# Window attention with a feed-forward layer on one core: six token tiles through DRAM instead of four, and a new table of the slices that carry scores, weight sums and saves

## The chip, the cores and the metric

One Trainium2 core does all of the work; the other cores of the chip stand idle. The time is the device time of one execution in microseconds. Three runs of the kernel before gave 850.49, 3289.97 and 848.82 us, and the median, 850.49 us, is its time. The program is written out in full for each engine: TensorE (PE) multiplies, VectorE (DVE), ScalarE (ACT) and GpSimd (POOL) work on tiles, and SyncE (SP) issues all DMAs. Each engine takes its instructions in the order in which the program names them, so an instruction that waits holds up all that stand behind it on its engine.

## The reference

Eight heads attend inside a window, four of them plain and four with dilation 4; a feed-forward layer with a leaky rectifier of its own slope for each hidden unit follows.

```python
B, H, S, D = 8, 8, 576, 64          # q, k, v are (8, 8, 576, 64)
scores = q @ k.T / sqrt(D)          # per batch and head
plain:   0 <= row - col < 32                                  (heads 0..3)
dilated: 0 <= row - col < 128 and (row - col) % 4 == 0         (heads 4..7)
attn = softmax(where(mask, scores, -1e9)) @ v
x = attn as (4608 tokens, 512)
h = x @ w_in                        # 512 -> 2048
g = max(h, 0) + alpha * min(h, 0)
out = g @ w_out                     # 2048 -> 512
```

## The kernel before, in words

The 4608 tokens form nine tiles of 512. Every fp32 operand of a big product is split into a high and a low part, and three passes (high by high, high by low, low by high) make one product.

**Two stages of the feed-forward layer.** Tiles 0 to 2 are done in 48 *slices*: slice n takes one tile and one block of 128 hidden units. In slice n TensorE does the input product of slice n+1 (line 488, `h`, 12 matmuls) and the output product of slice n-1 (line 536, `y`, 12 matmuls). Between them ScalarE and VectorE turn `h` into `m` (lines 496 and 501, or 508 and 509 on VectorE alone), then into its high part `g` (ACT, line 514) and its low part (DVE, line 519). Tiles 3 to 8 follow in a *paired stage*, which makes seven products out of eight (lines 729 and 1030) and needs sums of weight blocks for that. These sums are made during the slices: `combine` (line 586 and 589, POOL) for the input weights with its high part by ACT (line 594) and its low part by DVE (line 599), `others` (lines 616, 619, POOL; 624, ACT; 629, DVE) for the output weights. They are stored in DRAM, as are the plain weights (`save`, lines 568 to 572, four DMAs in each of 16 slices from `SCRATCH` on), and come back through a ring.

**The attention.** A *pair* is one batch element with two heads of one of four columns; there are 32. Pairs 8 to 23 are spread over the slices by the table `turns_at`: a pair's scores (PE line 266, 72 matmuls) are made in one slice, its values (PE line 361, 76 matmuls) in the slice of the next entry. Between the two stand the masks and maxima (DVE 318, 321), nine exponentials (ACT 331), the divisions (DVE 338, 339, 340) and the transpose into `pt` (DVE 346), which `values` waits for. The divisions stand in the slice after the scores. Where two entries are neighbours, all of that has one slice; else it has two. The result of `values` is copied to the token tiles, by ACT at lines 415 (between the fifth and the sixth exponential of the pair scored in that slice) and 422, for tiles 0 to 2 also by DVE (420).

**Where the tokens go.** For a tile in `KEPT` the copy goes to a small tile `kept_..` with the tag "m" (the five buffers of this tag also hold the `m` tiles, and the four output tiles `ob_..` of a token tile that is done), is stored to DRAM (line 225) and loaded again when its turn comes. Other tiles stay in SBUF (`raw_xA`, `raw_xB`). In the last slices `late_ops` prepare tiles 3 and 4 for the paired stage (`token_parts`: ACT 711, DVE 708 and 714).

**DMA.** SP issues every DMA in program order. The weights of the slices up to 21 are loaded by `load_weight` (line 435, tiles `ws`) in slices up to 18 and converted by ACT (457, 458, 473) and DVE (465, 467, 476). In slice 32 the output of token tile 0 is finished: four `ob` tiles are loaded with the first part (line 534), added to (DVE 544) and stored (line 549).

Of the kernel before, what the change touches and what calls it, by code (L numbers as in the profile page):

```python
# [8 lines left out]
F32 = mybir.dt.float32  # L9
# [8 lines left out]
P = 128  # L18
# [12 lines left out]
NTILE = NT // TT  # L31
NC = DM // P
NF = DFF // P
NSTD = 3
# [4 lines left out]
NRING = 10  # L39
HALF = 8  # L40
CUT = 6
KEPT = tuple(range(NSTD + 2, NTILE))
CHAINS = ((0, 5), (5, 5), (10, 4), (14, 4))


# [21 lines left out]
def tile_window_attention_prelu_ffn(  # L67
# [15 lines left out]
    const = ctx.enter_context(tc.tile_pool(name="const", bufs=1))  # L83
# [437 lines left out]
    def ffn_y(t, f):  # L521
        first = (t, f) in ((0, 0), (0, CUT), (1, 0), (2, HALF))
        if first:
            ys[t] = [bank("y", [P, TT], f"y_{t}_{f}_{c}") for c in range(NC)]
        g = gs.pop((t, f))
        cut, rest = (t, f) == (0, CUT - 1), t == 0 and f == NF - 1
        last = cut or (t, f) in ((0, NF - 1), (1, NF - 1), (2, HALF - 1))
        if last:
            o = [
                att.tile([P, TT], F32, tag=("k", "q", "v", "pt")[c], name=f"ob_{t}_{f}_{c}") if cut else  # L530
                ffp.tile([P, TT], F32, tag="m", name=f"ob_{t}_{f}_{c}", bufs=5) for c in range(NC)]
        for c in range(NC):
            if rest:
                nc.sync.dma_start(out=o[c], in_=part[c])
            for n, (a, e) in enumerate(PASSES):
                nc.tensor.matmul(  # L536
                    ys[t][c], lhsT=weight(1, a, f)[:, c * P:(c + 1) * P], rhs=g[:, e, :],
                    start=(first and n == 0), stop=(last and n == 2),
                )

        def end():
            for c in range(NC):
                if rest:
                    nc.vector.tensor_tensor(out=o[c], in0=ys[t][c], in1=o[c], op=ALU.add)
                elif c % 2:
                    nc.vector.tensor_copy(out=o[c], in_=ys[t][c])
                else:
                    nc.scalar.copy(out=o[c], in_=ys[t][c])
                nc.sync.dma_start(
                    out=part[c] if cut else outT[c * P:(c + 1) * P, t * TT:(t + 1) * TT], in_=o[c])  # L550

        if last:
            ended.append(end)
# [51 lines left out]

    wc = {}

    def others(i):

        if not ysums:  # L610
            ysums.append(const.tile([P, 2, 4, 2 * P], F32, tag="xA0", name="ysums"))
        t = ysums[0][:, len(ysums) % 2]
        ysums.append(t)
        for j in range(2):
            hi, lo = (weight(1, a, 2 * i + j).bitcast(F32) for a in range(2))
            nc.gpsimd.tensor_tensor(
                out=t[:, 2 * j:2 * j + 2].rearrange("p q n -> p (q n)"), in0=hi, in1=lo, op=ALU.add)
        for out, x, y, op in ((3, 1, 3, ALU.add), (1, 0, 1, ALU.subtract), (0, 3, 0, ALU.subtract), (2, 2, 0, ALU.subtract)):
            nc.gpsimd.tensor_tensor(out=t[:, out], in0=t[:, x], in1=t[:, y], op=op)
        sums_of[i] = t  # L620
# [13 lines left out]
                nc.sync.dma_start(  # L634
                    out=wY[i, q, :, :, a], in_=(t if a else t.bitcast(F32))[:, q].rearrange("p (c n) -> p c n", c=2))

    ysums = []
    sums_of = {}

    PRODUCTS = (1, 7, 6, 2, 5, 3, 4)  # L640
# [447 lines left out]

    def reload(t, c):
        tag = RAWTAGS[t]  # L1090
        if c == 0:
            cells.pop(tag, None)
            split.pop(tag, None)
        nc.sync.dma_start(out=half(t, c), in_=kept[t][c])
# [65 lines left out]
    def plan_parts():  # L1160
        zeroth, first, second = token_parts(NSTD)
        late_ops[NS - 9] = zeroth[:2]
        late_ops[NS - 5] = zeroth[2:] + first
        late_ops[NS - 3], late_ops[NS - 2], late_ops[NS - 1] = second[:5], second[5:8], second[8:]
# [3 lines left out]
    slices += [(2, f) for f in range(HALF, NF)] + [(2, f) for f in range(HALF)]  # L1168
    NS = len(slices)
    SECOND = CUT + NF  # L1170
    SCRATCH = CUT + NF - 2
    pairs = [Pair(b, c) for b in range(B) for c in range(NC)]


# [159 lines left out]
            ffn_y(*slices[n - 1])  # L1334

    score_at, value_at = {}, {}
    turns_at = (20, 22, 23, 24, 26, 27, 29, 30, 32, 33, 35, 36, 38, 40, 42, 44, 46)
    for p, (n, m) in enumerate(zip(turns_at, turns_at[1:]), 2 * NC):
        score_at[n] = pairs[p]
        value_at[m] = pairs[p]  # L1340
    divide_at = {n + 1: u for n, u in score_at.items()}

    split_at, combine_at = {}, {}
    for k, n in enumerate((21, 23, 25, 31, 33, 35, 37, 39)):
        combine_at[n] = (k + NFP // 2) % NFP
        split_at[n + 2] = combine_at[n]

    other_at, cast_at = {}, {}
    for k, n in zip((4, 5, 0, 1, 2, 3), range(32, 44, 2)):
        other_at[n] = cast_at[n + 2] = k  # L1350
    put = defaultdict(list)

    for n in range(CUT, NS):
# [69 lines left out]
        if n in cast_at:  # L1423
            others_low(cast_at[n])
            put[n + 1].append(lambda i=cast_at[n]: others_store(i))
        if n == HALF + 3:
            pairs[2 * NC].load_qk()
            pairs[2 * NC].load_v()
        for op in put.pop(n, ()):
# [3 lines left out]
        if n in combine_at:  # L1433
            combine(combine_at[n], "xB1" if n < 2 * NF - 1 else "xA1")
        if n in other_at:
            others(other_at[n])
        if n == NS - 9:
            plan_parts()
        if n == NS - 3:
            nc.sync.dma_start(out=mask_sb, in_=masks[:, NMASK:2 * NMASK])  # L1440
        for op in late_ops.pop(n, ()):
            op()
        if n >= NS - NRING + 2:
            feed()

    ffn_y(*slices[-1])
    ended.pop()()
    feed()
# [70 lines left out]
```

## Time and profile before

| what | us |
|---|---|
| runs | 850.49, 3289.97, 848.82 |
| median | 850.49 |
| the profiled execution | 849.21 |
| its span, first to last instruction | 846.7 |
| TensorE busy in the span | 823.8 (97%) |
| VectorE busy | 651.2 (77%) |
| ScalarE busy | 466.2 (55%) |
| GpSimd busy | 89.9 (11%), all but 0.2 of it from 163 us on to 363 us |

The slices 20 to 47 lie between about 163 and 363 us of the span, the paired stage behind them. A table by stretches of the span shows for each stretch how long each engine was busy; what TensorE is short of the stretch's length is time that it waited. A timeline row gives the start, the length, the engine, the line, the operation with the tile it writes and those it reads, and, in square brackets, how long the engine had been idle before it and what released it.

### The profile page before, as it was taken

The numbers are of one execution on the slowest core, as the hardware profiler recorded it, in microseconds if no ns is written. First come the engines' busy times: TensorE is split into PE (matmuls) and PEld (weight loads), VectorE is DVE, ScalarE is ACT, GpSimd is POOL, SyncE is SP. The second block draws the span as 40 slices with busy tenths as digits, with TensorE's granted clock in tenths as the row PEclk, the third lists the DMA queues.
The fourth block names the chain that finished last, engine by engine and source line by source line (L and its number), as shares of the span: only waits on it lengthen the run. The fifth ranks groups of instructions, "written<-read, shape, count | busy, mean of one in ns | idle before, by whom it ended". The sixth has DMA issues, their size and how long they took to land.

```text
span 846.7 us, 20417 instructions
## 1 busy us (share of the span) xinstructions
PE 823.8 (97%) x8014; PEld 670.0 (79%) x8014; DVE 651.2 (77%) x1088; ACT 466.2 (55%) x1275; POOL 89.9 (11%) x88
## 2 busy tenths in 40 slices
PE   8899999999999999999999999999999999999997
PEld 5677888887878777787888788878887888888886
DVE  5987767668668887879966999897289988934983
ACT  7885766554545655657436752665176436624640
POOL 0000000205054896000000000000000000000000
PEclk9999999999999999999999999999999999999999
DMA  7853444179889988695898599866876886767664
GB/s 256 273 176 112 131 163 148 45 250 303 274 256 301 289 272 261 189 298 167 260 317 300 158 323 302 259 185 198 250 212 193 288 291 192 194 193 195 191 195 150
DMA packets 137918, 190.71 MB, mean 225 GB/s; under 512 B 11870, under 2 KB 78046, under 8 KB 137822
## 3 DMA queue, kind: packets, MB, share of 16 engines
q1 hardware_dynamic: 137822, 189.41, 71.7%
q8 instruction: 63, 1.03, 0.5%
q14 instruction: 33, 0.27, 0.1%
HBM read 143.23 MB, written 46.14 MB: 224 GB/s over the span
## 4 chain that ended last, share of the span: by engine, by line
PE 79%; DVE 12%; ACT 4%; issue 2%; DMA 2%; SPq 0%; ACTq 0%; DVEq 0%
PE h L488 15%; PE qA L1030 15%; PE y L536 13%; PE pA L729 11%; PE qC L1030 7%; PE pC L729 6%; PE qB L1030 4%; PE pB L729 3%; PE o L361 3%; PE s L266 2%; ACT pr L331 2%; DVE held L788 1%; DVE pr L340 1%; DVE gp L843 1%; DVE stage L781 1%
## 5 line engine op out<-in xcount | busy, mean ns | idle before, releaser
L488 PE MATMUL h<-x,w_dt.float32r 128*128 128x512 f32 x576 | 143.5, 398 | 4.1 <-issue 1.7
L536 PE MATMUL y<-g,w_dt.float32r 128*128 128x512 f32 x576 | 138.5, 389 | 0.0
L488 PEld LDWEIGHTS h<-x,w_dt.float32r 128*128 128x128 f32 x576 | 107.6, 190 | 28.5 <-issue 2.6
L536 PEld LDWEIGHTS y<-g,w_dt.float32r 128*128 128x128 f32 x576 | 108.0, 188 | 22.5
L331 ACT ACTIVATE pr<-pr,nm 128x64 f32<-128x64 f32 x216 | 72.5, 339 | 33.5 <-DVE nm L321 30.7
L774 ACT COPY stage<-pA 128x512 f32<-128x512 f32 x72 | 42.3, 587 | 47.6 <-PE pA L729 46.9
L729 PE MATMUL pA<-parts_w,ring_w 128*128 128x512 f32 x234 | 58.1, 391 | 0.2 <-ACT stage L774 0.2
L838 ACT CAST gp<-held 128x512 fp32r<-128x512 f32 x60 | 37.2, 620 | 35.6 <-DVE held L834 35.3
L729 PE MATMUL pA<-parts_w,ring_xA 128*128 128x512 f32 x222 | 55.3, 393 | 0.7 <-ACT stage L774 0.7
L514 ACT CAST g<-m 128x512 fp32r<-128x512 f32 x48 | 29.7, 618 | 41.0 <-PE y L536 17.7
L729 PEld LDWEIGHTS pA<-parts_w,ring_w 128*128 128x128 f32 x234 | 43.6, 188 | 9.8 <-ACT stage L774 0.6
L519 DVE TENSOR_TENSOR g<-m,g 128x512 fp32r<-128x512 f32 x48 | 38.4, 800 | 15.3 <-ACT g L514 15.2
L729 PEld LDWEIGHTS pA<-parts_w,ring_xA 128*128 128x128 f32 x222 | 41.2, 188 | 10.5 <-ACT stage L774 1.9
L496 ACT ACTIVATE m<-h 128x512 f32<-128x512 f32 x32 | 19.1, 598 | 49.8 <-PE h L488 49.6
L781 DVE TENSOR_TENSOR stage<-pC,stage 128x512 f32<-128x512 f32 x48 | 32.9, 686 | 13.3 <-ACT stage L774 8.3
L955 ACT COPY py<-qA 128x512 f32<-128x512 f32 x24 | 13.8, 588 | 52.0 <-PE qA L1030 51.2
L1030 PE MATMUL qA<-gp,ring_xA 128*128 128x512 f32 x174 | 42.3, 389 | 0.0
L843 DVE TENSOR_TENSOR gp<-held,gp 128x512 fp32r<-128x512 f32 x60 | 40.5, 684 | 1.7 <-ACT gp L838 1.7
L331 ACT ACTIVATION_READ_ACCUMULATOR pr<-pr,nm 128x1 f32 x216 | 41.0, 190 | 0.0
L959 DVE TENSOR_TENSOR py<-qC,py 128x512 f32<-128x512 f32 x24 | 16.0, 687 | 31.0 <-PE qC L1030 24.8
L1030 PE MATMUL qA<-gp,ring_w 128*128 128x512 f32 x162 | 39.5, 389 | 0.0
L1030 PEld LDWEIGHTS qA<-gp,ring_xA 128*128 128x128 f32 x174 | 32.5, 188 | 7.0 <-DVE gp L843 0.4
(190 smaller groups left out, 1703.1 us busy)
## 6 DMA issues: line engine op xcount, KB each, us to landing
ring_w<-wS SPq DMA_DIRECT2D x69, 256.0 KB, 3.0
ring_xA<-wS SPq DMA_DIRECT2D x66, 256.0 KB, 3.2
ring_xA<-wY SPq DMA_DIRECT2D x40, 256.0 KB, 3.8
ring_w<-wY SPq DMA_DIRECT2D x36, 256.0 KB, 3.8
ring_g<-wS SPq DMA_DIRECT2D x33, 256.0 KB, 3.0
wO<-w_dt.float32r SPq DMA_DIRECT2D x32, 256.0 KB, 3.7
wS<-wc SPq DMA_DIRECT2D x16, 512.0 KB, 4.6
ring_w<-wO SPq DMA_DIRECT2D x31, 256.0 KB, 3.1
```

Of the source, the lines that this page charges most:

```text
L331: nc.scalar.activation(out=self.pr[:, r, :], in_=self.ps[r // CUT0][:, r % CUT0, :] if self.onto else self.pr[:, r, :], func=AF.Exp, bias= ...
L361: nc.tensor.matmul(self.po[u][e * D:(e + 1) * D, a:z, :], lhsT=self.v[rows, i, :], rhs=self.pt[rows, a * BK + (BQ if i else 0):z * BK - (B ...
L488: nc.tensor.matmul(ms[t, f], lhsT=weight(0, a, f)[:, c * P:(c + 1) * P], rhs=half(t, c)[:, e, :], start=(c == 0 and n == 0), stop=(c == NC ...
L514: nc.scalar.copy(out=g[:, 0, :], in_=ms[t, f])
L519: nc.vector.tensor_tensor(out=g[:, 1, :], in0=ms.pop((t, f)), in1=g[:, 0, :].bitcast(F32), op=ALU.subtract)
L536: nc.tensor.matmul(ys[t][c], lhsT=weight(1, a, f)[:, c * P:(c + 1) * P], rhs=g[:, e, :], start=(first and n == 0), stop=(last and n == 2),)
L729: nc.tensor.matmul(to, lhsT=w[:, (2 * a + c) * P:(2 * a + c + 1) * P], rhs=part_of(name, e)[:, c * TT:(c + 1) * TT], start=start and c == ...
L774: nc.scalar.copy(out=self.s(n), in_=self.A)
L781: nc.vector.tensor_tensor(out=self.s(n), in0=getattr(self, src), in1=self.s(to), op=ALU.add)
L838: nc.scalar.copy(out=self.pair(n)[:, 0], in_=self.whole(n))
L843: nc.vector.tensor_tensor(out=p[:, 1], in0=self.whole(n), in1=p[:, 0].bitcast(F32), op=ALU.subtract)
L1030: nc.tensor.matmul(to(q)[c], lhsT=w[:, k * P:(k + 1) * P], rhs=rhs[:, e], start=(i, q) in firsts and n == 0, stop=i == GP - 1 and n == 2, ...
```

## The change

- `KEPT` holds the tiles 3 to 8, where it held 5 to 8. So 16 more stores of kept tiles stand on SP (four pairs each for two tiles, at line 225), and eight loads that bring tile 3 (in slice 36) and tile 4 (in slice 40) back.
- `turns_at` begins at slice 17 instead of 20 and runs to 47 instead of 46. Neighbours before: 22/23/24, 26/27, 29/30, 32/33, 35/36. Neighbours now: 26/27, 29/30, 32/33. The first of these pairs is loaded in slice 9 instead of 11.
- `combine` stands in slices 21, 24, 27, 30, 33, 36, 39, 41 (before: 21, 23, 25, 31, 33, 35, 37, 39); its parts on ACT and DVE stand two slices behind, as before. `others` stands in 22, 25, 28, 32, 35, 38 (before: 32, 34, ... 42), its parts two slices behind; its sums lie in `xB0` up to slice 30, then in `xA0`.
- The 64 saves of plain weights stand in slices 12 to 27, where they stood in 20 to 35.
- The load of the mask stands one slice later, and the stores of the last kept tiles stand behind the loop.

```diff
-KEPT = tuple(range(NSTD + 2, NTILE))
+KEPT = tuple(range(NSTD, NTILE))
...
-    def others(i):
-
-        if not ysums:
-            ysums.append(const.tile([P, 2, 4, 2 * P], F32, tag="xA0", name="ysums"))
-        t = ysums[0][:, len(ysums) % 2]
-        ysums.append(t)
+    def others(i, tag):
+
+        if tag not in ysums:
+            ysums[tag] = const.tile([P, 2, 4, 2 * P], F32, tag=tag, name=f"ysums_{tag}")
+        t = ysums[tag][:, i % 2]
...
-    SCRATCH = CUT + NF - 2
+    SCRATCH = CUT + 6
...
-    turns_at = (20, 22, 23, 24, 26, 27, 29, 30, 32, 33, 35, 36, 38, 40, 42, 44, 46)
+    turns_at = (17, 20, 22, 24, 26, 27, 29, 30, 32, 33, 35, 37, 39, 41, 43, 45, 47)
...
-    for k, n in enumerate((21, 23, 25, 31, 33, 35, 37, 39)):
+    for k, n in enumerate((21, 24, 27, 30, 33, 36, 39, 41)):
...
-    for k, n in zip((4, 5, 0, 1, 2, 3), range(32, 44, 2)):
+    for k, n in zip((4, 5, 0, 1, 2, 3), (22, 25, 28, 32, 35, 38)):
...
-        if n == HALF + 3:
+        if n == HALF + 1:
             pairs[2 * NC].load_qk()
...
+        for t, at in ((NSTD, NS - 12), (NSTD + 1, NS - 8)):
+            for c in range(NC if n == at else 0):
+                reload(t, c)
         if n == NS - 9:
+            half(NSTD + 1, 0)
             plan_parts()
-        if n == NS - 3:
+        if n == NS - 2:
             nc.sync.dma_start(out=mask_sb, in_=masks[:, NMASK:2 * NMASK])
...
+    for op in put.pop(NS):
+        op()
```

On VectorE in slices 32 and 33, from the maxima of the pair that is scored in slice 32 to its transpose. Before:

```order
L318 SCALAR_TENSOR_TENSOR pr_78<-s_0_1_3302,mask_sb 128x256
L321 TENSOR_REDUCE nm_0_3385<-pr_78 128x4
L544 TENSOR_TENSOR ob_15_0_3281<-y_6_0_2273,ob_15_0_3281 128x512
L544 TENSOR_TENSOR ob_15_1_3282<-y_6_1_2274,ob_15_1_3282 128x512
L544 TENSOR_TENSOR ob_15_2_3283<-y_6_2_2275,ob_15_2_3283 128x512
L544 TENSOR_TENSOR ob_15_3_3284<-y_6_3_2276,ob_15_3_3284 128x512
L508 TENSOR_SCALAR m_10_3435<-h_10_3422,al 128x512
L509 SCALAR_TENSOR_TENSOR m_10_3435<-h_10_3422,m_10_3435 128x512
L338 TENSOR_SCALAR rs_0_3440<-sums_79 128x9
```

and now:

```order
L318 SCALAR_TENSOR_TENSOR pr_78<-s_0_1_3392,mask_sb 128x256
L321 TENSOR_REDUCE nm_0_3475<-pr_78 128x4
L544 TENSOR_TENSOR ob_15_0_3368<-y_6_0_2425,ob_15_0_3368 128x512
L544 TENSOR_TENSOR ob_15_1_3369<-y_6_1_2426,ob_15_1_3369 128x512
L544 TENSOR_TENSOR ob_15_2_3370<-y_6_2_2427,ob_15_2_3370 128x512
L544 TENSOR_TENSOR ob_15_3_3371<-y_6_3_2428,ob_15_3_3371 128x512
L599 TENSOR_TENSOR wc_1_3389<-wsum_xB_2235,wc_0_3388 128x1024
L508 TENSOR_SCALAR m_10_3526<-h_10_3513,al 128x512
L509 SCALAR_TENSOR_TENSOR m_10_3526<-h_10_3513,m_10_3526 128x512
L338 TENSOR_SCALAR rs_0_3531<-sums_79 128x9
```

The low part of a weight sum (L599) has come between the four output tiles and the `m` of the next slice. With more "m" tiles in use before this place, the tile `m_10` of line 508 now takes the buffer of the second output tile, `ob_15_1`, whose store it has to wait for; before it took one that had long been free.

On ScalarE in slice 32, the exponentials of the same pair with the copies of the pair whose values are made there. Before:

```order
L331 ACTIVATE pr_78,sums_79<-pr_78,nm_0_3385 128x64 x5
L415 COPY raw_xB_2234<-o_3_0_3343 128x80x2
L415 COPY raw_xB_2879<-o_3_0_3343 128x64x2
L331 ACTIVATE pr_78,sums_79<-pr_78,nm_0_3385 128x64 x4
L422 COPY raw_xB_2234<-o_3_1_3344 128x80x2
```

and now:

```order
L331 ACTIVATE pr_78,sums_79<-pr_78,nm_0_3475 128x64 x5
L415 COPY kept_3_3_3493<-o_3_0_3433 128x80x2
L415 COPY kept_3_3_3494<-o_3_0_3433 128x64x2
L331 ACTIVATE pr_78,sums_79<-pr_78,nm_0_3475 128x64 x4
L422 COPY kept_3_3_3493<-o_3_1_3434 128x80x2
```

The copies write tiles of the tag "m" now, and the second of them takes the buffer of the first output tile, `ob_15_0`; it waits for that tile's store, and the last four exponentials stand behind it.

On VectorE in slices 43 to 45 of the change, the late work on the tokens (L714, L708, L714, which are L713, L707, L713 in the changed file) beside the divisions and the transpose. Before:

```order
L340 TENSOR_TENSOR pr_78<-pr_78,rs_2_4564 128x576
L346 STREAM_TRANSPOSE pt_2_4568<-pr_78 128x576
L519 TENSOR_TENSOR g_4_4562<-m_4_4559,g_4_4562 128x512
L714 TENSOR_TENSOR parts_w_2_4593<-raw_xB_2234,parts_w_2_4593 128x1024
L708 TENSOR_TENSOR raw_xB_2234<-raw_xB_2879,raw_xB_2234 128x1024
L714 TENSOR_TENSOR parts_w_2_4597<-raw_xB_2234,parts_w_2_4597 128x1024
L501 SCALAR_TENSOR_TENSOR m_5_4614<-m_5_4614,bal,h_5_4601 128x512
```

and now:

```order
L599 TENSOR_TENSOR wc_1_4531<-wsum_xA_3659,wc_0_4530 128x1024
L713 TENSOR_TENSOR parts_w_2_4639<-raw_xB_3907,parts_w_2_4639 128x1024
L707 TENSOR_TENSOR raw_xB_3907<-raw_xB_4250,raw_xB_3907 128x1024
L713 TENSOR_TENSOR parts_w_2_4643<-raw_xB_3907,parts_w_2_4643 128x1024
L508 TENSOR_SCALAR m_5_4660<-h_5_4647,al 128x512
L509 SCALAR_TENSOR_TENSOR m_5_4660<-h_5_4647,m_5_4660 128x512
L338 TENSOR_SCALAR rs_2_4665<-sums_79 128x9
L339 RECIPROCAL rs_2_4665<-rs_2_4665 128x9
L340 TENSOR_TENSOR pr_78<-pr_78,rs_2_4665 128x576
L346 STREAM_TRANSPOSE pt_2_4669<-pr_78 128x576
L519 TENSOR_TENSOR g_5_4663<-m_5_4660,g_5_4663 128x512
L501 SCALAR_TENSOR_TENSOR m_6_4701<-m_6_4701,bal,h_6_4688 128x512
```

The late work has moved from behind the transpose to ahead of the divisions of the same pair; line 501, which also ends the use of the bank that the next values need, stands at the end of the row in both.

## Rows read from the trace of the kernel before

**Rows 1.** The page's first part: engine, busy us, share of the span, instructions.

```profile
PE 823.8 (97%) x8014; PEld 670.0 (79%) x8014; DVE 651.2 (77%) x1088; ACT 466.2 (55%) x1275; POOL 89.9 (11%) x88
```

**Rows 2.** Table by stretches: length, busy us per engine, clock, DMA share, GB/s.

```profile
163.00:363.00 200.00, 193.74 (x3030) 159.26 (x3029) 152.36 (x238) 106.23 (x407) 89.73 (x84) 1.00 0.84 260
...
126.00:136.00 10.00, 10.00 (x45) 8.28 (x45) 8.05 (x13) 5.64 (x11) 0.00 (x0) 1.00 0.53 159
...
240.00:280.00 40.00, 38.80 (x648) 32.02 (x649) 30.32 (x51) 20.41 (x86) 20.95 (x21) 1.00 0.92 288
```

**Rows 3.** Waits from 160 to 366 us: who, for whom, us, times, longest.

```profile
PE o L361 <- DVE pt L346: 2.5, 3, 1.1
...
PE h L488 <- issue: 1.7, 2, 1.5
PE h L488 <- DVE pr L318: 1.4, 3, 0.9
```

**Rows 4.** TensorE's timeline: three places where it had stood idle.

```profile
196.34 1.36 PE L361 MATMUL o<-pt,v 32*64 32x32 f32 x76 [1.11 <-DVE pt L346]
...
314.78 3.01 PE L488 MATMUL h<-x,w_dt.float32r 128*128 128x512 f32 x12 [0.86 <-DVE pr L318]
...
342.93 1.35 PE L361 MATMUL o<-pt,v 32*64 32x32 f32 x76 [0.52 <-DVE m L501]
```

**Rows 5.** Timeline, slice 27: divisions with nothing beside them.

```profile
216.29 0.76 DVE L340 TENSOR_TENSOR pr<-pr,rs 128x576 f32<-128x576 f32 x1
...
217.08 0.78 DVE L346 STREAM_TRANSPOSE pt<-pr 128x576 f32<-128x576 f32 x1
...
218.20 0.51 PE L361 MATMUL o<-pt,v 32*64 32x32 f32 x19
```

**Rows 6.** Timeline, slices 23 and 24: a weight sum ahead of the divisions.

```profile
190.98 1.22 DVE L599 TENSOR_TENSOR wc<-wsum_xB,wc 128x1024 fp32r<-128x1024 f32 x1
...
192.34 2.52 POOL L586 TENSOR_TENSOR wsum_xB<-w_dt.float32r 128x512 f32<-128x512 f32 x2 [23.43 <-DVE wc L599]
...
193.95 1.53 DVE L340 TENSOR_TENSOR pr<-pr,rs 128x576 f32<-128x576 f32 x1
```

**Rows 7.** Timeline, slices 32 and 33: the output tiles and the divisions.

```profile
255.89 2.47 DVE L544 TENSOR_TENSOR ob<-y,ob 128x512 f32<-128x512 f32 x4
...
256.60 3.92 SPq L549 DMA_DIRECT2D out<-ob  x4
...
256.96 0.44 ACT L415 COPY raw_xB<-o 128x160 f32<-128x160 f32 x2
...
258.63 0.45 ACT L422 COPY raw_xB<-o 128x160 f32<-128x160 f32 x2
...
258.98 0.75 DVE L508 TENSOR_SCALAR m<-h,al 128x512 f32<-128x512 f32 x1 [0.62 <-PE h L488]
...
262.73 0.98 PE L361 MATMUL o<-pt,v 32*64 32x32 f32 x51
```

**Rows 8.** The output tiles' stores: issue ns, first and last start, time to landing.

```profile
L549 SPq DMA_DIRECT2D out<-ob x4: 332/344/2127, 256.6 to 258.4; - x4
...
DMA to landing us min/median/max: 5.5/5.6/5.6
```

**Rows 9.** Kept tiles' stores: time to landing (the same view, 160 to 366 us).

```profile
DMA to landing us min/median/max: 1.6/4.0/4.4
```

**Rows 10.** Timeline, slices 43 and 44: the late work on the tokens.

```profile
339.91 1.05 ACT L711 CAST parts_w<-raw_xB 128x1024 fp32r<-128x1024 f32 x1 [2.42 <-DVE raw_xB L708]
...
340.99 1.23 DVE L714 TENSOR_TENSOR parts_w<-raw_xB,parts_w 128x1024 fp32r<-128x1024 f32 x1 [1.11 <-ACT parts_w L711]
```

**Rows 11.** Timeline, slices 16 to 18: the last weight loads and the last conversion.

```profile
143.51 4.02 SPq L435 DMA_DIRECT2D ws<-w_out  x2
...
152.58 0.68 ACT L457 ACTIVATE wa<-ws 128x512 f32<-128x512 bf16 x1
```

**Rows 12.** The page's part on DMA issues: count, KB each, us to landing.

```profile
wO<-w_dt.float32r SPq DMA_DIRECT2D x32, 256.0 KB, 3.7
```

More of the change, by code (lines that the diff above doesn't have):

```diff
@@ L635, in others_store @@
                     out=wY[i, q, :, :, a], in_=(t if a else t.bitcast(F32))[:, q].rearrange("p (c n) -> p c n", c=2))
-    ysums = []
+    ysums = {}
     sums_of = {}
@@ L1090, in reload @@
         tag = RAWTAGS[t]
-        if c == 0:
+        if c == 0 and t > NSTD + 1:
             cells.pop(tag, None)
@@ L1435, in tile_window_attention_prelu_ffn @@
         if n in other_at:
-            others(other_at[n])
+            others(other_at[n], "xB0" if n < 2 * NF - 1 else "xA0")
+        for t, at in ((NSTD, NS - 12), (NSTD + 1, NS - 8)):
+            for c in range(NC if n == at else 0):
+                reload(t, c)
         if n == NS - 9:
+            half(NSTD + 1, 0)
             plan_parts()
-        if n == NS - 3:
+        if n == NS - 2:
             nc.sync.dma_start(out=mask_sb, in_=masks[:, NMASK:2 * NMASK])
```

## The prediction, made before the changed kernel ran

> **What bounds the kernel now.** I read the busy shares first, then the table by stretches, then the waits and TensorE's timeline. The reader should see that TensorE is busy 823.8 of 846.7 us [rows 1]: nothing in the change alters its 8014 matmuls, so the change can only move the 23 us in which it stands. The stretch that the change touches, 163 to 363 us, holds 200.00 - 193.74 = 6.3 of these [rows 2]; slices before it show none (10.00 of 10.00 busy), and the paired stage behind it runs the same program. The 6.3 us have four causes [rows 3]: `values` waits for the transposed probabilities (2.5 us, three times), the next input product waits for the masks (1.4, three times), the instruction queue (1.7, twice), and once for `m` (0.5, the last of [rows 4]). The 2.5 us are neighbours in `turns_at`: a pair scored in one slice and valued in the next. So 6.3 us is the most that the change can win, 0.7% of the time; a difference of 2% (17 us), about what a measurement of this kernel tells from no change, can only come as a loss. The profiled execution took 849.21 us, 1.3 us below the median of 850.49; the sum is made against 849.21.
>
> **The price of a neighbour.** With nothing beside it, the division takes 0.76 us, the transpose 0.78 and ends at 217.86, and TensorE begins the values at 218.20 without having stood [rows 5]: 0.3 us to spare. In slices 23 and 24 the low part of a weight sum (1.22) stands ahead, GpSimd begins its next sum when that is done, and beside it the division takes 1.53 us [rows 6]; TensorE stood 1.11 us [first of rows 4]. So a neighbour with a weight sum split in its first slice costs about 1.1 us, one without costs nothing.
>
> Row first: beside GpSimd the division is 0.77 us longer, less than one GpSimd instruction of 1.26 (2.52 for two) [rows 5, 6]. The Trainium skill ("SBUF — State Buffer", "Who interferes with whom") says that a VectorE instruction with two SBUF inputs and a GpSimd instruction that reads SBUF lock each other out for a whole instruction. By that rule a division could lose all of 1.26 us; what that would give is the third rival.
>
> **The change, step by step.**
>
> *Scores from slice 17, saves from slice 12.* In slices 12 to 18 the masks, maxima and divisions of one pair come to a VectorE that is busy 8.05 of 10.00 us there [rows 2] (a slice has 24 of the 45 matmuls of these 10 us, 5.3 us). The 64 saves now pass the weight loads on SP: four per slice, 256 KB each, so 1.0 MB in 5.3 us, some 195 GB/s (an estimate) beside the 159 of this stretch [rows 2, 12]. The sum, some 355, is more than the 288 GB/s that the densest stretch shows. The last two loads are issued at 143.5 and by 147.5, and the last conversion begins at 152.58 [rows 11]; a converted weight is used about two slices behind, some 10.6 us. I put 0.3 us, between 0 and 3 (seven slices that each fall short by half a microsecond). The first neighbours, 22/23/24 and 35/36, go: the change takes away the 1.11 us of slice 24 and the 0.3 us or so of 36 (2.5 less two of about 1.1 [rows 3]).
>
> *Slices 26/27 and 29/30.* Both now have a split weight sum in the first slice and a new `combine` right behind, as 23/24 had. I take 1.1 for 26/27 and 0.7 for 29/30, which before cost up to 1.1 too [rows 3]. Ends: 0 and 1.5 each.
>
> *Slices 32/33.* This is the biggest term. Two things wait for a store that nothing waited for. The `m` of line 508 takes the buffer of `ob_15_1`, and a copy at line 415, with four exponentials behind it on ScalarE, that of `ob_15_0`. The stores are issued between 256.6 and 258.4 and land 5.5 us later [rows 8]: `ob_15_0` at 262.1, `ob_15_1`, next on SP, at about 262.7. Line 508 began at 258.98 [rows 7], so it comes 3.7 us later; from its end two VectorE steps of about 0.7 (509), 0.4 (338, 339) and the division and transpose (1.5) follow, so the values begin at about 262.7 + 0.75 + 0.7 + 0.4 + 1.5 + 0.4 = 266.4 where they began at 262.73. On ScalarE the copy moves from 256.96 to 262.1, and the four exponentials up to 258.63 [rows 7] go with it, to about 263.8; that is covered by the same wait. If the stores land as kept tiles do, in 4.0 us [rows 9], the loss is 2.2, since the saves are gone from this place. Against that, the loads of `ob` now stand on SP behind four stores of kept tiles and eight of weight sums, where four issues took 3.92 us [rows 7]. The sum takes 3; the ends are 1 (landings as short as the shortest kept store, 1.6 [rows 9]) and 6 (the first estimate plus 2 us of jam ahead of the loads). The 1.2 us of line 599, which is new here, ends before the store lands and is hidden as long as that wait is there.
>
> *Kept tiles 3 and 4.* 16 more stores of about 0.15 MB and eight loads of 0.25 MB, 4 MB in all over 24 slices, are on SP alone. Their copies replace copies of the same size. Nothing waits for the loads before slice 39, so the price is 0 beside what slices 32/33 pay.
>
> *Others from slice 22.* The same instructions, earlier; the queue of wY stores is thinned. The 0.86 us at slice 40 [rows 4], where masks came late behind a sum, go down to about 0.3.
>
> *Slices 43 to 47.* The lot of late token work (three VectorE instructions of 1.23 us with a wait of 1.11 for ScalarE's cast [rows 10], 4.8 us together) stood behind the transpose, where it cost 0.5 and then 0.4 us of TensorE [rows 3, 4]; it now stands ahead of the divisions, and its cast behind the nine exponentials of the same pair. The path from the scores to the values has two slices, four input or output products of 2.7 us with the scores and values of two pairs. On it I count in the timeline of slices 43 and 44, from the start of the scores: maxima done at 2.7 us, exponentials to 6.6, cast 7.7, the rest of the lot to 11.2, `m`, divisions and low part 4.2 to 15.4, and line 501 (0.74), which the values wait for, to 16.2; they could begin at 14.7. So 1.5 and 0.4 for the masks behind it: 1.9 instead of 0.9. The lot of slice 45 comes to the same place, where before none was waited for: 1.9, ends 0 and 2.5.
>
> *The instruction queue.* 1.7 as before; the ends are 0 and 3.
>
> **Sum.** Now: 0.3 + 1.1 + 0.7 + 3 + 0.3 + 1.9 + 1.9 + 1.7 = 10.9. Before: 6.3. So 4.6 us more: 849.2 + 4.6 = 853.8, and I say 853.5, since two of the terms are patterns that a small shift of the engines against each other may hide.
>
> **Rivals.**
>
> *The change does what its table looks like* (0.25). The neighbours' stalls go, the stores land early because the saves are gone, and ScalarE's cast slips in between exponentials. For it: the DMA share in the dense stretch is 0.92 [rows 2], and the change takes 8 MB of saves out of it. Against it: the two buffers are really the output tiles'. Then 2 to 4 of the 6.3 us are left, and the time is 849.2 - 4.3 to 849.2 - 2.3, about 845 to 847.
>
> *The weights come too late* (slower, 0.05). The saves stand ahead of the weight loads in slices 12 to 18 and the sum of 355 GB/s is above what the stretches show. Short by 67 GB/s for seven slices of 5.3 us is 2.5 MB, at 288 GB/s about 9 us; less the slack of two slices nothing is lost, and that is why it is a rival only. It decides as soon as the conversion's own chain (load, ScalarE, VectorE, ScalarE, VectorE over two slices) uses the slack up: then each of the seven slices gives TensorE a gap of about 2.5 us, 17 together, and with the 4.6 of the sum the time is about 870.
>
> *GpSimd locks VectorE out* (0.1). In slices 27, 30 and 33 a division would wait for a whole GpSimd instruction, 1.26 instead of 0.77, and the low part behind it (519) again: about 1 us more at each, 3 in all, 856.5. This is what the page named above would give; the rows so far show the smaller figure.
>
> *The queue jams around slice 32* (0.1). Then `ob` loads, stores and kept tiles are late one behind the other, and the stall is 6 to 10 instead of 3: 857 to 861.
>
> My own case has 0.5: 850 to 857.
>
> **Numbers.** The likeliest time is 853.5. From 845.5 to 860 the first rival's upper part, my own case, the third and most of the fourth lie inside: 0.8 or a little more. Faster by over 2% would need 17 us of the 6.3 that are there: 0.01. Slower by over 2% (867) needs the second rival nearly whole: 0.03. Within 2%: 0.96.
>
> **What would show it.** Right: after the change TensorE waits at slice 33 for `pt` by 2 us or more, with line 508 or ScalarE's copy released by the DMA of `out`; at slices 45 and 47 it waits for `m` or `pt` behind 713. Wrong: no idle time of TensorE at slice 33, or TensorE idle before input products of slices 13 to 20, released by conversions. The stretch from slice 20 to the paired stage should hold 9 to 13 us of TensorE's idle time; if it holds 2 to 4, the first rival is right.

## The result, and the profile after

The changed kernel takes 855.6 us (median of 7 runs, 852.66 to 857.62) where the kernel before took 848.82 (7 runs on the same chip). The ratio is 1.0075, with a 95% interval of 1.0052 to 1.0098: slower by less than one per cent, inside the range of 845.5 to 860, and 2 us above the forecast of 853.5. The profiled execution took 855.94 us, its span was 853.9, 7.2 more than before.

The first part of the page after, and the table by stretches (length, busy time of PE, PEld, DVE, ACT and POOL with their instructions, granted clock, DMA share, GB/s), answer to [rows 1, 2]:

```profile
PE 827.2 (97%) x8014; PEld 673.6 (79%) x8014; DVE 653.2 (76%) x1087; ACT 466.8 (55%) x1276; POOL 87.2 (10%) x88
```

```profile
163.00:363.00 200.00, 190.97 (x2878) 157.85 (x2877) 146.36 (x225) 100.43 (x383) 86.99 (x84) 0.99 0.75 236
...
270.00:280.00 10.00, 10.00 (x75) 8.30 (x69) 6.13 (x12) 5.40 (x23) 0.00 (x0) 0.84 0.32 97
```

TensorE was idle for 9.0 of the 200 us where it had been idle for 6.3, and in the ten microseconds from 270 on the granted clock was 0.84. All of its idle time between slice 17 and the first scores of the paired stage stands in these rows of its timeline (start, length, operation, and in brackets the idle time before it with what ended it); they answer to [rows 3, 4]:

```profile
198.17 3.04 PE L488 MATMUL h<-x,w_dt.float32r 128*128 128x512 f32 x12 [0.17 <-DVE pr L318]
...
219.62 1.21 PE L266 MATMUL s<-k,q 64*32 64x64 f32 x72 [2.16 <-DMA q<-qT]
...
242.63 1.36 PE L361 MATMUL o<-pt,v 32*64 32x32 f32 x76 [0.18 <-DVE pt L346]
...
258.72 3.03 PE L488 MATMUL h<-x,w_dt.float32r 128*128 128x512 f32 x12 [1.19 <-DVE pr L318]
...
269.09 1.88 PE L361 MATMUL o<-pt,v 32*64 32x32 f32 x76 [3.14 <-DVE pt L346]
...
326.54 3.03 PE L488 MATMUL h<-x,w_dt.float32r 128*128 128x512 f32 x12 [0.42 <-DVE pr L318]
...
353.62 1.35 PE L361 MATMUL o<-pt,v 32*64 32x32 f32 x76 [1.22 <-DVE m L501]
...
355.40 3.02 PE L488 MATMUL h<-x,w_dt.float32r 128*128 128x512 f32 x12 [0.42 <-DVE pr L318]
...
365.53 1.35 PE L361 MATMUL o<-pt,v 32*64 32x32 f32 x76 [1.68 <-DVE pt L346]
...
371.76 0.86 PE L290 MATMUL s<-lasting_k,lasting_q 64*32 64x64 f32 x64 [0.34 <-DVE ob L546]
```

They sum to 10.9 us, the figure of the prediction's sum. The places are those of this one profile. Up to slice 42 the program of e3 below is that of the changed kernel, and its profile has 1.65 us at slice 27 instead of 2.16, 0.88 at 30 instead of 0.18, 0.38 at 32 instead of 1.19, and 3.15 at 33 instead of 3.14: the small waits are known to about 1 us, the large one repeats.

The 7.2 us of the spans divide as follows. At a place ahead of everything that was changed, the last wait of the first stage (values at 66.11 us before, at 67.63 after), the run was already 1.5 us behind: start-up differs from run to run, and in the profiles below the same place lies between 64.6 and 69.1 us. From the scores of slice 20 (165.58 before, 168.44 after) to the first product of the paired stage (362.66 and 369.65) 4.1 us were lost; the scores of slice 17 (1.1) no longer lie in that stretch, so it holds 5.3 us more. Idle time is 10.6 there instead of 6.2, which is 4.4 of them. The slower clock behind slice 33 has some 1.6 more, a wait inside the scores of slice 33 has 0.3 (both in the rows below), and some 1 us in the other direction I can't place.

Slice 33, where the longest wait is, on three engines and on SP (the stores' issues, the scores, the copy into the kept tile, line 508, the input product behind the values), with the stores' time to landing from the view of the output tiles:

```profile
260.59 2.12 SPq L549 DMA_DIRECT2D out<-ob  x4
...
264.40 1.55 PE L266 MATMUL s<-k,q 64*32 64x64 f32 x72
...
264.97 0.27 ACT L415 COPY kept<-o 128x128 f32<-128x128 f32 x1 [3.44 <-DMA out<-ob]
...
265.62 0.75 DVE L508 TENSOR_SCALAR m<-h,al 128x512 f32<-128x512 f32 x1 [1.87 <-DMA out<-ob]
...
270.90 4.04 PE L488 MATMUL h<-x,w_dt.float32r 128*128 128x512 f32 x12
...
DMA to landing us min/median/max: 4.3/4.3/4.4
```

Against [rows 7, 8]: the copy waited 3.44 us for the store of `ob_15_0`, line 508 waited 1.87 us for that of `ob_15_1`, and the values came 3.14 us late. The stores landed 4.3 us behind their issue, between the two figures (5.5 and 4.0) from which the term was bounded. The input product behind the values took 4.04 us instead of 3.02. From the scores of slice 33 to those of slice 35 it was 13.54 us before (261.59 to 275.13) and 18.63 after (264.40 to 283.03): 5.09 more. The wait is 3.14 of it. The values (1.88 instead of 1.35) and the product (4.04 instead of 3.02) have 1.55, at the slower clock. The scores took 1.55 instead of 1.21 with the clock still at 1.00: their second half waited 0.3 us for ScalarE's copy.

Slice 27 waited for `q`. SP's rows ahead of it:

```profile
205.83 2.72 SPq L633 DMA_DIRECT2D wY<-wd  x4
...
208.65 2.56 SPq L633 DMA_DIRECT2D wY<-ysums_xB  x4
...
211.91 1.84 SPq L572 DMA_DIRECT2D wO<-w_dt.float32r  x1
...
215.43 0.53 SPq L237 DMA_DIRECT2D q<-qT  x1
```

Two lots of four wY stores and the saves of slice 25 stand ahead of the load of `q`, which was issued at 215.43, 6 us behind the start of the scores of slice 26 (209.30), which free its room, and landed 4.1 us later.

Slices 43 to 47, VectorE's rows of the late work, which answer to [rows 10]:

```profile
344.31 1.23 DVE L713 TENSOR_TENSOR parts_w<-raw_xB,parts_w 128x1024 fp32r<-128x1024 f32 x1 [2.88 <-ACT parts_w L710]
...
347.79 1.23 DVE L713 TENSOR_TENSOR parts_w<-raw_xB,parts_w 128x1024 fp32r<-128x1024 f32 x1 [1.12 <-ACT parts_w L710]
...
360.73 1.22 DVE L713 TENSOR_TENSOR parts_w<-raw_xB,parts_w 128x1024 fp32r<-128x1024 f32 x1 [1.80 <-ACT parts_w L710]
```

VectorE stood 2.88, 1.12 and 1.80 us ahead of the divisions. The first and the third time it waited for a cast that ScalarE makes behind the exponentials, the second time for a cast that itself had to wait for VectorE's line 707.

### The profile page after: what moved, and what is told of

Its sections match the earlier page's. It is cut to its first block, busy times and chain, and to the rows that moved or that the text cites. A ratio compares the mean times of both kernels' runs of the same rounds, so it can differ in the third digit from the quotient of the medians.

```text
span 853.9 us, 20465 instructions
## 1 busy us (share of the span) xinstructions
PE 827.2 (97%) x8014; PEld 673.6 (79%) x8014; DVE 653.2 (76%) x1087; ACT 466.8 (55%) x1276; POOL 87.2 (10%) x88
## 4 chain that ended last, share of the span: by engine, by line
PE 74%; DVE 12%; ACT 6%; DMA 4%; issue 3%; SPq 2%; DVEq 0%; ACTq 0%
PE qA L1029 14%; PE h L488 11%; PE pA L728 11%; PE y L536 11%; PE qC L1029 7%; PE pC L728 5%; PE qB L1029 4%; ACT pr L331 3%; PE pB L728 3%; PE o L361 3%; PE s L266 2%; DVE held L787 1%; PE idle L127 1%; DMA out<-ob 1%; SPq L633 1%
## 5 line engine op out<-in xcount | busy, mean ns | idle before, releaser
L519 DVE TENSOR_TENSOR g<-m,g 128x512 fp32r<-128x512 f32 x48 | 41.1, 856 | 15.1 <-ACT g L514 15.1
L728 PEld LDWEIGHTS pA<-parts_w,ring_xA 128*128 128x128 f32 x222 | 41.2, 188 | 10.6 <-ACT stage L773 2.0
```

The lines of the kernel that those rows point to most:

```text
L519: nc.vector.tensor_tensor(out=g[:, 1, :], in0=ms.pop((t, f)), in1=g[:, 0, :].bitcast(F32), op=ALU.subtract)
L728: nc.tensor.matmul(to, lhsT=w[:, (2 * a + c) * P:(2 * a + c + 1) * P], rhs=part_of(name, e)[:, c * TT:(c + 1) * TT], start=start and c == ...
```

## The experiments

Each was compared with runs of the kernel before on its own chip; the ratios are to these, and the changed kernel's is 1.0075. "Changed kernel" is the kernel after the change.

### A room of its own for the output tiles (e1_ob_room)

```diff
+            if rest:
+                room = const.tile([P, NC, TT], F32, tag="xA1", name=f"ob_{t}_{f}")
+                o = [room[:, c] for c in range(NC)]
```

> The four output tiles of slice 32 lie in a room of their own (xA1) instead of the tag m, so nothing waits for their stores. Theory (buffers): the 3.14 us of TensorE's idle time at slice 33 go down to 1.1 or less (a neighbour with a weight sum in front), the 3.4 us wait of ScalarE's copy and the 1.9 us wait of line 508 for the store are gone, and with the stall goes the dip of the granted clock (0.84 in 270 to 280 us), which cost some 1.9 us: 3.5 to 5 us faster than the changed kernel, about 851. Rival (queue): SP and the DMA engines are late there anyway, the wait moves to another transfer: 855 or more, and idle time of 2 us or more at slice 33. Rival on the clock: the dip has another cause and stays at 0.9 or less in that stretch; then only 2 to 3 us are won.

It took 851.27 us, ratio 1.0021 (1.0003 to 1.0039), against 1.0075 about 4.6 us less. Nothing waits for the stores any more, but part of the wait moved to the loads:

```profile
251.53 3.22 SPq L537 DMA_DIRECT2D ob<-part  x4
...
259.85 0.69 DVE L547 TENSOR_TENSOR ob<-y,ob 128x512 f32<-128x512 f32 x1 [1.17 <-DMA ob<-part]
...
265.06 1.36 PE L361 MATMUL o<-pt,v 32*64 32x32 f32 x76 [2.33 <-DVE pt L346]
```

The four loads of the first parts are issued behind eight wY stores, VectorE waits 0.51, 0.87 and 1.17 us for them before it can add the output tiles, and the values of slice 33 still come 2.33 us late. Both theories have a share: without the shared buffers the wait is 0.8 us shorter and the scores take 1.21 us again, and behind the wait for the stores stood another one of 2.3, that for the loads. The granted clock is 1.00 from 60 to 840 us, and the values behind the 2.33 us take 1.36 us as ever.

### The wY stores one slice later (e2_wy_later)

```diff
-            put[n + 1].append(lambda i=cast_at[n]: others_store(i))
+            put[n + 2].append(lambda i=cast_at[n]: others_store(i))
```

> The eight stores of each weight sum wY are issued one slice later, behind the loads of k, q and v for the next pair. Theory (SP's queue): the 2.16 us that the scores of slice 27 waited for q go away, but the division of slice 27 is still slow beside GpSimd, so about 1 us comes back as a wait for pt: 1 us faster than the changed kernel. Rival (memory traffic): the transfers are slow because the DMA engines are full, whatever SP issues first; q still lands 4.2 us behind its issue and the scores wait 1.5 us or more: no difference.

852.39 us, ratio 1.0046 (1.0028 to 1.0063): about 2.5 us less than the changed kernel, where 1 us was expected; the two intervals still touch. `q` is there in time, and the values wait 0.74 for the division instead:

```profile
220.14 1.36 PE L361 MATMUL o<-pt,v 32*64 32x32 f32 x76 [0.74 <-DVE pt L346]
...
267.72 1.36 PE L361 MATMUL o<-pt,v 32*64 32x32 f32 x76 [2.48 <-DVE pt L346]
```

So the order on SP made `q` late, not the amount of traffic; this place gives back 1.2 of the 2.5 us (2.16 less 0.74 and 0.17). Slice 33 still waited 2.48, though here the clock did not fall behind it.

### The late work on tokens cut (e3_late_cut)

```diff
-        late_ops[NS - 5] = zeroth[2:] + first
-        late_ops[NS - 3], late_ops[NS - 2], late_ops[NS - 1] = second[:5], second[5:8], second[8:]
+        late_ops[NS - 5] = zeroth[2:3]
+        late_ops[NS - 4] = zeroth[3:] + first[:2]
+        late_ops[NS - 3], late_ops[NS - 2], late_ops[NS - 1] = first[2:] + second[:4], second[4:8], second[8:]
```

> The late work on tokens is cut so that VectorE takes no low part in the slice in which its cast is queued behind exponentials (the lot of slice 43 mostly in 44, that of 45 mostly in 46, behind the transposes). Theory (late work ahead of the divisions): the idle times 1.22 + 0.42 at slice 45 and 1.68 at slice 47 go to 0.5 together, and the paired stage starts at most 0.7 later against its first product: 2 to 3 us faster than the changed kernel. Rival: line 501 and pt are late for another reason (the exponentials of a pair, which end 6.6 us behind its scores), and the stalls stay above 2 us together: same time.

852.12 us, ratio 1.0039 (1.0023 to 1.0054), about 3.1 us less, again with intervals that touch. The three stalls of slices 45 and 47 (3.3 us) are gone, and TensorE goes from slice 43 to the paired stage without a pause; 1.16 us at its first scores is what is left:

```profile
350.77 1.35 PE L361 MATMUL o<-pt,v 32*64 32x32 f32 x76
...
360.45 1.35 PE L361 MATMUL o<-pt,v 32*64 32x32 f32 x76
...
367.51 0.86 PE L290 MATMUL s<-lasting_k,lasting_q 64*32 64x64 f32 x64 [1.16 <-DVE ob L546]
```

The exponentials were not what held up the values: it was the low parts that waited for casts behind them.

### The weight sums split in the second of two neighbours (e8_sums_behind)

```diff
-    for k, n in enumerate((21, 24, 27, 30, 33, 36, 39, 41)):
+    for k, n in enumerate((22, 25, 28, 31, 34, 36, 39, 41)):
```

> The weight sums of GpSimd are placed so that their split (line 599) falls into slices 24, 27, 30, 33, 36, 38, 41, 43, the second of two neighbours, instead of 23, 26, 29, 32, .... Theory (GpSimd beside the division): the division of slices 27, 30 and 33 takes 0.76 us again, the 1.19 us at slice 32 (masks late behind a 1.71 us low part beside GpSimd) go to 0.3, the wait for q at slice 27 and the wait for the output stores at 33 stay: 1 us faster than the changed kernel. Rival (lock for whole instructions matters more): up to 3 us faster. Rival (sums are off the path): same, and the stall at slice 32 stays.

860.39 us, ratio 1.0134 (1.0101 to 1.0167), 5 us more than the changed kernel: no theory had that. The splits now fall into the slices of the casts of `others`, so that the two wS and the eight wY stores of slices 25 and 31 both stand on SP ahead of the loads that slices 27 and 32 wait for:

```profile
220.50 1.21 PE L266 MATMUL s<-k,q 64*32 64x64 f32 x72 [3.53 <-DMA q<-qT]
...
255.91 3.62 SPq L633 DMA_DIRECT2D wY<-ysums_xB  x4
...
269.81 0.27 ACT L415 COPY kept<-o 128x128 f32<-128x128 f32 x1 [7.06 <-DMA out<-ob]
...
273.93 2.35 PE L361 MATMUL o<-pt,v 32*64 32x32 f32 x76 [3.15 <-DVE pt L346]
```

`q` of slice 27 is 3.53 us late (2.16 before this edit), the loads of the output tiles are issued at 259.57, and ScalarE's copy waits 7.06 us for the store of the first. What was expected of the divisions came in the main (0.76 us at slices 27 and 33, 1.11 at 30), and the wait of 1.19 at slice 32 is gone, but GpSimd's place matters less here than what its results do to SP's queue.

### The old turns in the changed kernel, and the new turns in the kernel before (e4_old_turns, e5_new_turns)

```diff
-    turns_at = (17, 20, 22, 24, 26, 27, 29, 30, 32, 33, 35, 37, 39, 41, 43, 45, 47)
+    turns_at = (20, 22, 23, 24, 26, 27, 29, 30, 32, 33, 35, 36, 38, 40, 42, 44, 46)
...
```

> The changed kernel with the old table of turns (20, 22, 23, 24, ... 46); kept tiles, sums and saves stay as changed. Theory (each part pays at its own place): the stalls at slices 45 and 47 (1.22, 0.42, 1.68) shrink to about 1, since the late work stands behind the transposes again; the wait for the output stores at slice 33 stays at 2.5 us or more, since the buffers belong to the kept tiles; slices 23, 24 and 36 cost up to 1 us each again: 853 to 856, the changed kernel's time within 2 us. Rival (the turns are what costs): 850 or less and no long wait at slice 33.

860.12 us, ratio 1.0112 (1.0054 to 1.017): above the 853 to 856 expected, though the interval takes in the changed kernel's 1.0075. The wait at slice 33 stays, as it should if the kept tiles own it. Slice 23 costs 2.50 us and a slower clock behind it, where up to 1 us was expected, and its cause is the same: line 508 waits 2.73 us for the store of an output tile. The kernel before has no wait there, and in the changed kernel slice 23 carries no values. The waits of the late work (slices 45 and 47 in the changed kernel, 44 here) shrink from 3.3 to 1.6:

```profile
186.75 0.75 DVE L508 TENSOR_SCALAR m<-h,al 128x512 f32<-128x512 f32 x1 [2.73 <-DMA out<-ob]
...
190.22 2.34 PE L361 MATMUL o<-pt,v 32*64 32x32 f32 x76 [2.50 <-DVE pt L346]
...
272.81 2.35 PE L361 MATMUL o<-pt,v 32*64 32x32 f32 x76 [3.12 <-DVE pt L346]
...
354.17 1.35 PE L361 MATMUL o<-pt,v 32*64 32x32 f32 x76 [1.18 <-DVE m L501]
```

> The kernel before with the new table of turns alone (first pair loaded in slice 9, mask one slice later); kept tiles 5 to 8, sums and saves as before. Theory: the stalls of slices 24, 36 and 40 go (2.3 us), 29/30 stays near 1, those of the late work at slices 45 and 47 come (3.3 instead of 0.9): 848 to 850.5, the same as before. Rival (neighbours are what bounds these slices): 2 us or more faster than before, 846.5 or less.

856.22 us, ratio 1.0079 (1.0053 to 1.0106): 7 us slower than the kernel before, where no difference was expected. Most neighbours' stalls are gone, but with the old slices of the weight sums the late work on tokens hits the values of slices 41 and 45:

```profile
321.14 1.90 PE L361 MATMUL o<-pt,v 32*64 32x32 f32 x76 [2.12 <-DVE m L501]
...
352.90 2.35 PE L361 MATMUL o<-pt,v 32*64 32x32 f32 x76 [2.88 <-DVE m L501]
...
342.45 1.22 DVE L714 TENSOR_TENSOR parts_w<-raw_xB,parts_w 128x1024 fp32r<-128x1024 f32 x1 [4.02 <-ACT parts_w L711]
...
373.46 0.86 PE L290 MATMUL s<-lasting_k,lasting_q 64*32 64x64 f32 x64 [2.07 <-DVE ob L546]
```

There VectorE waits 4.02 us for a cast behind the exponentials, and the low part of a wY sum (line 629) follows ahead of line 501. The values come 2.12 and 2.88 us late, both times with a slower clock behind them, and the paired stage's first scores 2.07 late. So the late work is what the new turns cost: in the changed kernel e3 shows it, here the rows say so and no run takes it away. My price of 3.3 was too low here.

### The saves, back in the changed kernel and alone in the kernel before (e7_old_saves, e6_new_saves)

```diff
-    SCRATCH = CUT + 6
+    SCRATCH = CUT + NF - 2
```

> The changed kernel with the saves of plain weights in slices 20 to 35 again. Theory (SP's queue around slices 27 and 32 is what makes the transfers late): four more issues per slice stand ahead of the loads of q and of the output tiles in slices 28 to 35, the waits at slices 32 and 33 grow: 2 to 5 us slower than the changed kernel, 857 to 860. Rival (saves beside the weight loads cost something): TensorE has no idle time in slices 12 to 20 in the changed kernel, so nothing is won; a time below 854 would speak for it.

863.99 us, ratio 1.0169 (1.013 to 1.0208): some 8 us more than the changed kernel, and more than the 857 to 860 expected. The saves stand ahead of the loads again:

```profile
241.89 2.15 PE L266 MATMUL s<-k,q 64*32 64x64 f32 x72 [3.47 <-DMA q<-qT]
...
265.46 4.65 PE L536 MATMUL y<-g,w_dt.float32r 128*128 128x512 f32 x12 [2.21 <-DVE ob L544]
...
275.83 2.20 PE L361 MATMUL o<-pt,v 32*64 32x32 f32 x76 [3.16 <-DVE pt L346]
```

`q` of slice 30 is 3.47 us late, the output tiles 2.21, and slice 33 waits 3.16 as before. Behind each of the three the granted clock was lower (0.83 in the ten microseconds from 240, from 260 and from 270 on), so part of the 8 us is the clock.

> The kernel before with the saves of plain weights in slices 12 to 27 and nothing else. Theory (saves beside the weight loads hide, TensorE does not wait in slices 12 to 20): the same time as before, within 1.5 us, 847.5 to 850. Rival (SP's queue bounds slices 28 to 36 before, too): 1.5 us or more faster. Rival (weights come late): idle time of TensorE before input products in slices 13 to 20, 3 us or more slower.

848.24 us, ratio 0.9995 (0.9983 to 1.0007): no difference. TensorE was not idle in slices 12 to 20, so the saves beside the weight loads hide. The stalls of the kernel before stay at their places (1.12 at 24, 1.06 at 30); only 36 grew to 0.88. Moving the saves is thus free by itself, and worth about 8 us once the other parts of the change have filled SP's queue.

### Three mends together (e9_mend, e10_mend2, e11_split27)

The first has the output tiles' loads ahead of slice 31's stores in `xA1`, the later wY stores of e2 and the cut late work of e3:

```diff
...
+        if whole:
+            room = const.tile([P, NC, TT], F32, tag="xA1", name="ob_early")
+            early.extend(room[:, c] for c in range(NC))
+            for c in range(NC):
+                nc.sync.dma_start(out=early[c], in_=part[c])
...
```

> Three mends in one: the output tiles of slice 32 in a room of their own with their loads ahead of slice 31's stores, the wY stores one slice later, and the late work on tokens cut. Theory: of the 10.9 us of TensorE's idle time from slice 17 on, those at 27 (2.2 to 0.9), 32 and 33 (4.3 to 1.2) and 45 to 47 (3.3 to 0.3) go down, and the dip of the clock behind slice 33 (1.9 us) stays away: 7 to 9 us faster than the changed kernel, 846.5 to 848.5, at or just below the kernel before. Rival: what is taken away at one place comes back at the next (the weight sums' low parts, the paired stage's first products), 850 or more.

849.81 us, ratio 1.0007 (0.9983 to 1.0031), short of the 846.5 to 848.5 expected. Slice 33 waits 0.22 us instead of 3.14, but the later store of a wY sum holds the buffer of `wd`, which a cast of `g` needs, and 2.63 us come back one slice on with a slow product behind them:

```profile
264.25 1.36 PE L361 MATMUL o<-pt,v 32*64 32x32 f32 x76 [0.22 <-DVE pt L346]
...
266.18 0.62 ACT L515 CAST g<-m 128x512 fp32r<-128x512 f32 x1 [5.72 <-DMA wY<-wd]
...
268.24 4.50 PE L489 MATMUL h<-x,w_dt.float32r 128*128 128x512 f32 x12 [2.63 <-DVE pr L318]
```

The second has the same mends, but delays only the stores of slice 25:

```diff
...
-            put[n + 2].append(lambda i=cast_at[n]: others_store(i))
+            put[n + (2 if n == 24 else 1)].append(lambda i=cast_at[n]: others_store(i))
...
```

> The three mends again, but only the wY stores of slice 25 are issued one slice later; those of slice 31 and later stay where they were, behind the early loads of the output tiles. Theory (the later wY store held the buffer of wd, so that the cast of g waited 2.63 us for it on ScalarE at slice 34, and the clock fell behind that): this stall and the dip of the clock go, 2.63 + 1.5 us: 845 to 847, 2 to 4 us faster than the kernel before. Rival (a full SP queue at 31 to 34 whatever the order): the wait moves to the loads of k and q for slice 33 or to the output tiles' stores, and the time stays at 849 to 851.

846.02 us (7 runs), ratio 0.9967 (0.9949 to 0.9985): it beats both kernels, the one before by 2.8 us and the changed one by about 9. What is left of TensorE's idle time, apart from five waits of 0.42 or less:

```profile
197.72 3.02 PE L489 MATMUL h<-x,w_dt.float32r 128*128 128x512 f32 x12 [0.56 <-DVE pr L318]
...
218.85 1.36 PE L361 MATMUL o<-pt,v 32*64 32x32 f32 x76 [0.71 <-DVE pt L346]
...
319.79 3.02 PE L489 MATMUL h<-x,w_dt.float32r 128*128 128x512 f32 x12 [0.36 <-DVE pr L318]
...
362.31 0.86 PE L290 MATMUL s<-lasting_k,lasting_q 64*32 64x64 f32 x64 [1.16 <-DVE ob L547]
```

Its granted clock is 1.00 in every ten microseconds from slice 20 to 840 us.

The third splits the weight sum of slice 24 in slice 27 instead of 26:

```diff
-        split_at[n + 2] = combine_at[n]
+        split_at[n + (3 if n == 24 else 2)] = combine_at[n]
```

> As e10_mend2, and the weight sum of slice 24 is split in slice 27 instead of 26, so that GpSimd begins its next sum behind the division of slice 27. Theory: the division of slice 27 takes 0.76 us instead of 1.54, and the 0.74 + 0.17 us of idle time there go: 0.5 to 1 us faster than e10_mend2. Rival (GpSimd then runs beside the next neighbours, 29/30): same time or slower.

847.8 us, ratio 0.9982 (0.9966 to 0.9998), not told apart from the second. The division of slice 27 takes 0.76 us and the wait there (0.71 + 0.18) is gone; but the two wS stores now stand on SP with the eight wY stores between the loads for slice 29 and those for slice 30, and `q` of slice 30 is 3.28 us late:

```profile
214.72 0.76 DVE L340 TENSOR_TENSOR pr<-pr,rs 128x576 f32<-128x576 f32 x1
...
240.47 1.21 PE L266 MATMUL s<-k,q 64*32 64x64 f32 x72 [3.28 <-DMA q<-qT]
```

This prices GpSimd beside the division at slice 27: 0.9 us, near the 1.1 that the prediction took for these neighbours.

## Why the prediction was right, point by point

**The path.** The idle time of TensorE was the place to look, and the signs named beforehand came: 3.14 us ahead of the values of slice 33 with line 508 and ScalarE's copy released by the stores of `out`, waits for `m` and `pt` behind line 713, and 10.6 us between slice 20 and the paired stage (9 to 13 forecast). That the sums agree to a tenth, 10.9 and 10.9, is luck: slices 26/27, slice 32 and some small waits brought about 3 us more than forecast, and 29/30, the late work, the saves and the instruction queue about 3 us less. The slower clock (1.6 us) was not in the sum at all.

**Slices 32/33 (3, range 1 to 6): 3.14.** Mechanism and size of the wait were right: line 508 waited for its store, and its steps to the transpose followed. But the buffers alone are worth less than 3. Taking them away (e1) removed the wait for the stores and uncovered one of 2.33 for the loads behind it; with both taken away (e9) 0.22 is left. So the jam on SP ahead of the loads, which was kept as an upper end and a rival, is real too, and e7 and e8 make it worse.

**Late work (1.9 + 1.9): 1.64 + 1.68.** Right, with the reason: e3 took all of it away. That the same lots would cost about 7 us of waits in the kernel before with the new turns (e5: 2.12, 0.33, 2.88 and 2.07) I had not reckoned.

**Slices 26/27 (1.1) and 29/30 (0.7): 2.16 and 0.18.** The step by which a weight sum split in the first slice makes the division slow holds (1.54 us in the changed kernel, 0.76 in e11), but at 27 the load of `q` came still later and hid it. The prediction named the queue of SP only for slice 32; it should have counted what stands ahead of every load of `q`, as e2 shows.

**Slice 32: 1.19, forecast nothing.** The masks of slice 32 came behind a division of 1.55 us and a low part of 1.71 beside GpSimd. That is the same mechanism at a pair that has two slices; I priced it only for neighbours. The size is uncertain: the same program had 0.38 there in e3.

**Saves (0.3), wY from slice 22 (0.3), the instruction queue (1.7): 0, 0.42 and 0.** The saves are free in slices 12 to 20 (e6). Issue waits of 0.2 to 1.5 us come and go from run to run (1.7 in the kernel before, none in the changed one): a term that a sum should carry as noise.

**The rivals.** The first, a gain, failed at the buffers and at the late work: the waits that left (24, 36, the issue waits) were replaced. The second, weights too late, did not occur: TensorE was busy 10.00 of 10.00 us in each ten microseconds from 100 to 160, though 349 GB/s moved in the last of them, more than the 288 that the prediction took for the most; and a quarter of the saves have 128 KB, where it counted 256 for each. The fourth, the jam, occurred in part. For the third the rows show: the division goes from 0.76 (e11) to 1.54 us beside GpSimd, 0.78 more, and `rs` (line 338) in e8 from 0.16 to 1.24 in slice 30:

```profile
242.43 1.24 DVE L338 TENSOR_SCALAR rs<-sums 128x9 f32<-128x9 f32 x1
```

The rule of the Trainium skill ("SBUF — State Buffer", "Who interferes with whom") that one of the two waits for a whole instruction of the other agrees with this as a bound: no VectorE instruction between 160 and 366 us of these profiles lost more than 1.18 us (line 519, 0.65 to 1.82, e7), less than one GpSimd instruction of 1.26 us. It did not make the 3 us of the rival, since at slice 33 GpSimd was not yet running and at 27 the wait was hidden.

**Not settled.** The 1 us that the balance leaves over, how far the waits below 1 us repeat, and why some of the long waits are followed by a slower clock and others not.

## What to carry to other kernels

When a change sends more tiles through a rotating set of buffers, list for each tile whose buffer it takes and what still reads it: here the store of a tile that had itself been loaded behind twelve other stores stopped two engines. On a queue that issues in order, look at what stands ahead of every load: with the wY stores of 128 KB moved behind the loads that the next slice needs the kernel was 2.5 us faster (e2), and with the saves eight slices earlier some 8 (e7), but a store that is moved back keeps its source buffer longer (e9). And work that needs a cast from a second engine belongs behind the point where that engine's long list ends.

## What the runs showed that was not expected

A wait of TensorE can cost more than its length. Behind 3.14 us at slice 33 the granted clock was 0.84 over ten microseconds and 0.50 in the three from 270 to 273, so TensorE ran there at the lower of its two levels, 1.2 instead of 2.4 GHz, and the values and the product took 1.55 us longer. The same followed waits of 2.50 and 3.12 (values 2.34 and 2.35 us instead of 1.35, e4), 3.15 (2.12, e3), 3.53 and 3.15 (2.34 and 2.35, e8), 3.47, 2.21 and 3.16 (scores 2.15 instead of 1.21, a product of 4.65 instead of 2.88, values 2.20, e7), 2.12 and 2.88 (1.90 and 2.35, e5) and 2.63 (a product of 4.50 instead of 3.02, e9). It did not follow 2.07 (e5), 2.16 (changed kernel, slice 27), 2.33 (e1), 2.48 (e2) and 3.28 (e11, scores 1.21 as ever). Most of the longer waits were followed by it, but 2.12 was and 3.28 was not, so the length of a wait alone does not decide it; what does, these runs do not show.
